# Planning a gated attention and MLP kernel again: modelled buffer slots, score bursts on distinct row tiles, copies from the first, one Gelu per batch

## The chip, the cores and the metric

The kernel runs on one core of one Trainium2 chip. The metric is the device time of one execution in microseconds (us). An engine is named as the profile names it: PE is the matmul engine, ACT is ScalarE, DVE is VectorE, POOL is GpSimd, SP is the engine that issues most DMAs.

## The reference, cut to what matters

```python
# x: 2048 x 512 (bf16), 32 heads of 16, F = 1792
qkv = (x @ wqkv) ...                                  # q, k, v per head
scores = einsum("bhqd,bhkd->bhqk", q, k) * 16 ** -0.5
a = einsum("bhqk,bhkd->bhqd", softmax(scores), v) ... @ wo

h  = gelu(layernorm(x) @ w1)                          # first Gelu batch
x1 = x + concat(four quarters of h, shifted by 1, -1, 2, -2 rows) @ w2
b  = x1 + gelu(layernorm(x1) @ w3) @ w4               # four more batches, one per 512 rows

g  = sigmoid((x * gate_w).sum(-1))
out = g * a + (1 - g) * b
```

Softmax over 32 heads x 2048 x 2048 scores is the bulk of the work. A *score tile* is 128 keys x 512 queries of one head; there are 2048 of them, handled in 32 rounds of 64 (a round is a chunk `c` of 512 queries, a group `G` of eight heads, and the even or odd heads `p` of the group). Each tile needs a small score matmul, an exp, and P·V matmuls that are collected in one accumulator, `acc`, in PSUM, the memory that PE writes to.

## The kernel before

The order of every instruction is planned at build time by an event model inside the kernel, the class `Sim`. It has one queue per engine, a duration and a latency for every job, and counts of free buffers. In this text "the planner" is that model. Once the chip runs, each engine works through its list in the planned order, so a wrong latency in the planner can't be corrected at run time.

Two parts matter here. The first is how a score tile becomes weights for P·V. Most tiles go to ACT as bursts of three or two tiles. About a quarter go to DVE, which builds an approximate exp from the bits: one pass `p1`, then two shifted copies on DVE and one on POOL. A tile done this way needs four P·V matmuls instead of one.

```python
def issue_act(got, cls):                      # 3 or 2 score tiles in one PSUM buffer
    ...
        nc.scalar.activation(out=box["p"][:, 0:n], in_=get()[:, 0:n], func=ACT.Exp, scale=0.25)

def act_tiles(n):                             # which tiles: distinct row groups within one burst
    for r in range(acc_round[0], min(NR, acc_round[0] + 3)):
        for x in left[r]:
            ...
            if any(g[1][1] == x[1] for g in got):
                continue
            got.append((r, x))
            if len(got) == n:
                return got

def close_pair(pr):                           # two DVE tiles together, 1024 wide
    ...
    for k in range(1, 4):
        def sh(k=k):
            d = pr["box"]["d"]
            if k < 3:                         # copy k reads copy k - 1
                nc.vector.tensor_scalar(out=d[:, k, 0:w], in0=d[:, k - 1, 0:w], scalar1=float(SHIFT), ...)
            else:
                nc.gpsimd.tensor_scalar(out=d[:, k, 0:w], in0=d[:, k - 1, 0:w], ...)
        j = dve(0.26 * w + 72.0, last, sh, prio=1) if k < 3 else gp(..., last, sh, prio=1)
        last = [j]
```

The second is the Gelu. It is cut into four instructions per batch, each with the previous one as a dependency, and only the first is charged with a table load by the planner:

```python
for m in range(KT):                           # first batch: KT = 4
    ge.append(act(1800 + (1300 if m == 0 else 0), pre + ge, lambda m=m: nc.scalar.activation(
        out=hT["h"][:, m, 2:2 + S], in_=hT["h"][:, m, 2:2 + S], func=ACT.Gelu_apprx_tanh), prio=0))
...
for q, (a, b) in enumerate(((0, 4), (4, 8), (8, 11), (11, 14))):    # in each of four chunks
    ge.append(act(93 + 427 * (b - a) + (1300 if q == 0 else 0), pre + ge, ...Gelu of box["h"][:, a:b, :]))
```

The third is the planner's constants, the buffer pools, and the gate, which writes one number per row to DRAM and reads it back in another layout:

```python
class Sim:
    SWITCH = 95.0
    ISSUE = 27.0
    PE_LAT = 220.0
...
NPA, NPD = 5, 3                               # exp results; DVE quadruples of [P, 4, 1024]
oDp = pool("oDp", 2)                          # attention output, [P, 4, 512] for a whole chunk c
...
d1 = dma(2200.0, [a], lambda: nc.sync.dma_start(out=zE_dram[:].rearrange("(t p) -> p t", p=P), in_=zE[:]))
...
# end of a round: acc -> accsb, its denominators -> den -> pk, then on DVE
r1 = dve(230, [d1], lambda: nc.vector.reciprocal(out=box["k"][:], in_=box["k"][:]), prio=0)
r2 = dve(90, [r1] + jg[1], ...pk * gpk...)    # gpk is the gate, read back from zE_dram
```

The softmax here doesn't subtract the row's maximum and nothing guards it: scores larger than these inputs give would overflow.

Of the kernel before, what the change touches and what calls it, by code (L numbers as in the profile page):

```python
# [18 lines left out]
SHIFT = 32  # L19
# [21 lines left out]
class Buf:  # L41
    def __init__(self, cls, users):
        self.cls, self.users = cls, users
# [34 lines left out]
class Sim:  # L78
    SWITCH = 95.0
    ISSUE = 27.0  # L80
    PE_LAT = 220.0

    def __init__(self, counts):
        self.free = dict(counts)
        self.jobs = {e: [] for e in ("ACT", "DVE", "POOL", "SP")}
        self.t_free = {e: 0.0 for e in ("ACT", "DVE", "POOL", "SP", "PE")}
        self.t = 0.0
        self.events = []
        self.n = 0
        self.order = []  # L90
        self.mode = None
        self.arr = [0.0] * 4
        self.tiles = 0
        self.pending = 0
        self.busy = {e: 0.0 for e in self.t_free}
        self.stat = {}
        self.log = []

# [10 lines left out]

    def release(self, bufs):  # L110
        for b in bufs:
            b.users -= 1
            if b.users == 0:
                self.free[b.cls] += 1
# [10 lines left out]
    def try_engine(self, e):  # L125
# [3 lines left out]
        for j in self.jobs[e]:  # L129
# [6 lines left out]
            if any(self.free[b.cls] <= 0 for b in j.acq):  # L136
                continue
# [7 lines left out]
        for b in j.acq:  # L145
            self.free[b.cls] -= 1
# [10 lines left out]
    def pe_run(self, ops):  # L157
        cur = self.t
        for o in ops:
# [11 lines left out]
            o.start = s  # L171
            cur = s
# [16 lines left out]
    def run(self, pe_pick, done):  # L189
# [17 lines left out]
        if not done():  # L207
            raise RuntimeError(f"the model of the engines stopped at {self.t}: {self.free} {self.tiles} {[(j.name,len(j.deps)) for e in self.jobs for j in self.jobs[e]][:20]}")
# [3 lines left out]
def kernel(  # L212
# [26 lines left out]
    COL = True  # L239

    NPA, NPD = 5, 3
    pool = lambda name, bufs, **kw: ctx.enter_context(tc.tile_pool(name=name, bufs=bufs, **kw))
    const = pool("const", 1)
    wpool = pool("wpool", 4)
    qpool = pool("qpool", 2)
    bigp = pool("bigp", 1)
    xnTp = pool("xnTp", 2)
    xnp = pool("xnp", 4)
    pap = pool("pap", NPA)
    pdp = pool("pdp", NPD)  # L250
    accp = pool("accp", 2)
    oTp = pool("oTp", 2)
    oDp = pool("oDp", 2)
    otp = pool("otp", 2)
    smallp = pool("smallp", 3)
    psA = pool("psA", 1, space=bass.MemoryType.PSUM)
    psR = pool("psR", 2, space=bass.MemoryType.PSUM)
    psC = pool("psC", 1, space=bass.MemoryType.PSUM)
    dpool = pool("dram", 1, space=bass.MemoryType.DRAM)
    drr = pool("drr", 3, space=bass.MemoryType.DRAM)  # L260
# [3 lines left out]


    x_sb = const.tile([P, NT, D], BF16, name="x_sb")
    xT = const.tile([P, KT, S], BF16, name="xT")
    wq = const.tile([P, KT, D], BF16, name="wq")
    wo = const.tile([P, KT, D], BF16, name="wo")
    w3 = const.tile([P, KT, F], BF16, name="w3")  # L270
    kT = [const.tile([P, S], BF16, name=f"kT{g}") for g in range(4)]
    V0 = const.tile([P, NT, 4, 4, 2, DH + 1], BF16, name="V0")
    V2 = const.tile([P, NT, 4, 2, 2, DH + 1], BF16, name="V2")
    gw = const.tile([P, KT], BF16, name="gw")
    mE = const.tile([P, 1], F32, name="mE")
    mO = const.tile([P, 1], F32, name="mO")
    mhalf = const.tile([P, NT], F32, name="mhalf")
    omg = const.tile([P, NT], F32, name="omg")
# [4 lines left out]
    nm = [const.tile([P, NT], F32, name=f"nm{i}") for i in range(2)]  # L283
    xn_dram = dpool.tile([2, S, D], BF16, name="xn_dram")
# [5 lines left out]
    sim = Sim({"psA3": 1, "psA2": 1, "ring": 2, "acc": 1, "PA": NPA, "PD": NPD, "xnT": 2, "xn": 4, "accsb": 2, "bcs": 2,  # L290
               "oT": 2, "q": 2, "qf": 2, "big": 1, "ot": 2, "small": 3, "w": 4, "oD": 2})
# [16 lines left out]
    wts = {}  # L308

    def wload(name, src, c0=0, c1=None):  # L310
        def fn():
            wts[name] = wpool.tile([P, KT, D], BF16, tag="w", name="w_" + name)
            n = src.shape[0] // P
            nc.sync.dma_start(out=wts[name][:, 0:n, :], in_=wrows(src))
        return fn

    wk_t = wpool.tile([P, KT, D], BF16, tag="w", name="w_k")
    wts["k"] = wk_t
    sim.free["w"] -= 1
    for c0, c1 in ((0, 128), (128, 512)):  # L320
        nc.scalar.dma_start(out=wk_t[:, :, c0:c1], in_=wrows(A_wqkv[:, D + c0:D + c1]))
        nc.scalar.dma_start(out=wq[:, :, c0:c1], in_=wrows(A_wqkv[:, c0:c1]))
    wv_t = wpool.tile([P, KT, D], BF16, tag="w", name="w_v")
    wts["v"] = wv_t
    sim.free["w"] -= 1
    nc.scalar.dma_start(out=wv_t[:], in_=wrows(A_wqkv[:, 2 * D:3 * D]))
    nc.scalar.dma_start(out=gw[:], in_=gate_w.rearrange("(kt p) -> p kt", p=P))
    dl_w = {"k": sim.add(Job("SP", 1, 5000.0, [], None)), "v": sim.add(Job("SP", 1, 9000.0, [], None))}

    gp(150, [], lambda: nc.gpsimd.memset(mhalf[:], -0.5), prio=0)  # L330

    mi = const.tile([P, 1], mybir.dt.int32, name="mi")
    mb = const.tile([P, 1], mybir.dt.int32, name="mb")
    gp(200, [], lambda: nc.gpsimd.iota(mi[:], pattern=[[0, 1]], base=0, channel_multiplier=1), prio=0)
    j_io = sim.jobs["POOL"][-1]
# [6 lines left out]
    gp(700, [], lambda: nc.gpsimd.memset(V0[:, :, :, :, :, 0:1], 1.0), prio=1)  # L342
    j_v1 = sim.jobs["POOL"][-1]

    acc = psC.tile([P, 512], F32, name="acc")
    j_acc0 = dve(550, [], lambda: nc.vector.memset(acc[:], 1.0), prio=0)

    j_xT = {}
    for c in range(NCH):
        for k in range(KT):  # L350
            j_xT[c, k] = dma(2600.0 + 300.0 * k, [], lambda c=c, k=k: nc.sync.dma_start(  # L351
                out=xT[:, k, c * 512:(c + 1) * 512], in_=x_by_d[c * 512:(c + 1) * 512, k], transpose=True), prio=0)
    j_x = []
    for c in range(NCH):
        j_x.append(dma(4000.0, [], lambda c=c: nc.sync.dma_start(
            out=x_sb[:, 4 * c:4 * c + 4, :], in_=x_flat[c * 512:(c + 1) * 512, :].rearrange("(t p) d -> p t d", p=P)),
            prio=1))
    bw = {}
    for name, src in (("1", B_w1), ("2", B_w2)):
        bw[name] = Buf("w", 0)  # L360
        dl_w[name] = dma(5000.0, [], wload(name, src), prio=2, acq=[bw[name]])
    dl_w["o"] = dma(5000.0, [], lambda: nc.sync.dma_start(out=wo[:], in_=wrows(A_wo)), prio=2)
    dl_w["3"] = dma(9000.0, [], lambda: nc.sync.dma_start(out=w3[:], in_=wrows(B_w3)), prio=2)
# [4 lines left out]
    def gen(name, at, deps, mms, N=512, M=P):  # L368

        box = {}  # L370

        def get():
            if "ps" not in box:
                box["ps"] = psR.tile([P, 512], F32, tag="ring", name="ring")
            return box["ps"]

# [11 lines left out]
        g.get = get  # L388
# [3 lines left out]
    def evac(g, hold, fn, prio=2, eng="DVE", **kw):  # L392
        job = Job(eng, hold, 150.0, [g.units[-1][-1]] if not COL else g.units[-1], lambda: fn(g.get()), prio=prio,
                  frees=[g.buf] + kw.pop("frees", []), **kw)
        return sim.add(job)
# [6 lines left out]
    def k_proj(G, c, at):  # L402
        g = gen(f"k{G}", at, [j_xT[c, k] for k in range(KT)] + [dl_w["k"]],
                [(lambda a, b, k=k: wts["k"][:, k, G * P + a:G * P + b],
                  lambda k=k: xT[:, k, c * 512:(c + 1) * 512]) for k in range(KT)])
# [4 lines left out]
    qt = {}  # L410
    j_q = {}

    qbuf = {}

    def q_proj(G, c, at):
        g = gen(f"q{G}", at, [j_xT[c, k] for k in range(KT)] + [dl_w["k"]],
                [(lambda a, b, k=k: wq[:, k, G * P + a:G * P + b],
                  lambda k=k: xT[:, k, c * 512:(c + 1) * 512]) for k in range(KT)])
        box = {}
        qfb = Buf("qf", 2)  # L420

        def cp(ps):
            box["f"] = qpool.tile([P, 512], BF16, tag="qf", name="qf")
            nc.vector.tensor_copy(out=box["f"][:], in_=ps[:])

        e = evac(g, PSUM_NS, cp, prio=1, acq=[qfb])
        qb = Buf("q", 128)
        qbuf[G, c] = qb
        js = []
        for p, m in ((0, mE), (1, mO)):  # L430
            def mk(p=p, m=m):
                if p == 0:
                    qt[G, c] = qpool.tile([P, 2, 512], BF16, tag="q", name="q")
                nc.gpsimd.tensor_scalar(out=qt[G, c][:, p, :], in0=box["f"][:], scalar1=m[:], scalar2=1.0,
                                        op0=ALU.mult, op1=ALU.mult)
            js.append(gp(680, [e, j_m3] + js, mk, prio=0, acq=[qb] if p == 0 else [], frees=[qfb]))
        j_q[G, c] = js
# [4 lines left out]
    def v_proj(t, at):  # L442
        c = t // 4
        g = gen("v", at, [j_xT[c, k] for k in range(KT)] + [dl_w["v"]],
                [(lambda a, b, k=k: xT[:, k, t * P + a:t * P + b], lambda k=k: wts["v"][:, k, :]) for k in range(KT)])
        j_v[t] = evac(g, PSUM_NS, lambda ps: nc.vector.tensor_copy(  # L446
            out=V0[:, t, :, :, :, 1:DH + 1], in_=ps[:].rearrange("p (g i o d) -> p g i o d", g=4, i=4, o=2)), prio=2)
        e = t % 2
        j_v2[t] = gp(480, [j_v[t], j_v1], lambda: nc.gpsimd.tensor_scalar(
            out=V2[:, t], in0=V0[:, t, :, e::2, :, :], scalar1=W2, scalar2=1.0, op0=ALU.mult, op1=ALU.mult), prio=1)  # L450


    def gate(at):
        g = gen("z", at, [j_xT[c, k] for c in range(NCH) for k in range(KT)], [], M=P)
# [683 lines left out]
```

## Time and profile before

| before | |
|---|---|
| time, median of its 4 runs beside the result | 954.03 us (951.48 to 961.69) |
| ACT busy / PE busy in the profiled run | 807.8 / 832.3 of 951.6 us |
| table loads on ACT | 41, of 1283 ns |
| ACT idle up to its last exp | 120.1 us |
| PE slots used by the 2048 score matmuls | 1016, of which 379 with one matmul |

The idle time of ACT is summed from the gaps between its instructions in the trace, and 807.8 + 120.1 + 23.8 us after the last exp gives the span, but for rounding. A *score slot*, or PE slot, is a group of score matmuls that start less than 60 ns after one another, because they use different row tiles of the array and run side by side; it is not one of the buffer slots below.

The profile page of the kernel before has the busy time of each engine, the busy tenths in 40 slices with the PE clock that was granted (PEclk, in tenths of full clock; "half clock" below is a stretch in which half was granted), and the chain of work that ended last.

```profile
PE 832.3 (87%) x8949; PEld 258.6 (27%) x8949; DVE 715.2 (75%) x1338; ACT 807.8 (85%) x680; POOL 386.9 (41%) x405
...
PE   4996899997789989978999987999959999979982
...
ACT  0665999999889999998979899799998889999990
...
PEclk9997999998799999976979997999968999969996
...
PE 51%; ACT 16%; DVE 16%; issue 8%; DMA 3%; SPq 3%; POOL 2%; ACTq 0%; POOLq 0%; DVEq 0%
```

No engine is full over the whole span. ACT does almost nothing in the first slice (23.8 us); afterwards ACT and PE take turns at 9. In the table of stretches (start:end, length, then the busy us of PE, PE weight load, DVE, ACT, POOL with their instructions, PE clock, DMA share, GB/s) the two regimes of the kernel before stand side by side:

```profile
192.00:240.00 48.00, 37.64 (x384) 10.91 (x381) 35.55 (x69) 46.54 (x39) 20.06 (x20) 0.93 0.09 27
...
480.00:528.00 48.00, 47.85 (x637) 16.95 (x633) 29.50 (x56) 39.90 (x34) 15.29 (x14) 0.93 0.10 27
```

In the first ACT is full (46.5 of 48), in the second PE is (47.9 of 48). Anything taken from ACT should pay at once in the first and not in the second. The groups of the kernel before by shape (line, engine, operation, shapes, count, then busy us and mean ns, then idle time just before and its releasers) show what fills ACT, and the DVE copies:

```profile
L732 ACT ACTIVATE PA<-psA 128x1536 bf16<-128x1536 f32 x309 | 452.5, 1464 | 75.4 <-PE psA L673 62.4 <-PE acc L820 9.0 <-PE ring L673 1.9
...
L792 DVE TENSOR_SCALAR PD<-PD 128x1024 uint16<-128x1024 uint16 x502 | 252.3, 503 | 10.6
...
L732 ACT ACT_TABLE_LOAD x21 | 26.9, 1283 | 11.3 <-DMA wq<-in_A_wqkv_dram 11.0
...
L600 ACT ACT_TABLE_LOAD x16 | 20.5, 1283 | 0.3
...
L557 ACT ACT_TABLE_LOAD x4 | 5.1, 1283 | 0.1
```

The three rows of loads are 21 + 16 + 4 = 41, or 52.6 us: 20 to a Gelu, 20 back to exp, and one at the start. The timeline of ACT (start, duration, engine, line, operation, count) in the kernel before shows why there are so many:

```profile
409.51 1.28 ACT L600 ACT_TABLE_LOAD   x1
410.81 1.91 ACT L600 ACTIVATE h<-h 128x2048 bf16<-128x2048 bf16 x1
412.74 1.28 ACT L732 ACT_TABLE_LOAD   x1
414.03 1.02 ACT L732 ACTIVATE PA<-psA 128x1024 bf16<-128x1024 f32 x1
415.07 1.28 ACT L600 ACT_TABLE_LOAD   x1
```

Between two quarters of one Gelu batch the planner slips a single exp of 1.02 us, and that costs two loads, 2.56 us. The code explains it: a quarter counts as finished 160 ns after it leaves ACT, so when ACT comes free the next quarter isn't ready yet, an exp is, and the planner does not charge the loads that this brings.

The waits of ACT for scores and P·V before (engine, tile and line, what was waited for: us in total, times, longest) come to 73.3 + 26.9 + 3.9 = 104 us; the page's own total for the exp, with small items, is 107.1 us.

```profile
ACT PA L732 <- PE psA L673: 73.3, 91, 12.1
ACT PA L732 <- PE acc L820: 26.9, 22, 3.5
...
ACT PA L732 <- PE ring L673: 3.9, 10, 0.9
```

Last, two places of the timeline before: the first exp, and one pair of shifted copies on DVE.

```profile
24.33 2.36 ACT L732 ACTIVATE PA<-psA 128x1536 bf16<-128x1536 f32 x2 [12.07 <-PE psA L673]
...
305.34 0.96 DVE L792 TENSOR_SCALAR PD<-PD 128x1024 uint16<-128x1024 uint16 x2
```

### The profile page before, as it was taken

What the parts mean: (1) busy time and instruction counts of PE and PEld (TensorE: products, weight loads), DVE (VectorE), ACT (ScalarE), POOL (GpSimd) and SP (SyncE); (2) the same over time, 40 slices, a digit from 0 to 9 for tenths busy, and PEclk for the clock granted to TensorE, in tenths of its full rate; (3) what the DMA queues carried; (4) which work ended last, traced back from release to release, by engine and by line L of the source; (5) the groups of instructions that cost most, each with busy time, mean ns of one, the idle gap of its engine ahead of it and who ended that gap; (6) DMA issues with size and microseconds to landing.
All of it is one profiled execution on the core that took longest, in us unless ns stands there. A gap on an engine that the chain in (4) does not pass through costs nothing.

```text
span 951.6 us, 22237 instructions
## 1 busy us (share of the span) xinstructions
PE 832.3 (87%) x8949; PEld 258.6 (27%) x8949; DVE 715.2 (75%) x1338; ACT 807.8 (85%) x680; POOL 386.9 (41%) x405
## 2 busy tenths in 40 slices
PE   4996899997789989978999987999959999979982
PEld 1341232322222223311223322332312333223220
DVE  1775988887699998856966785788848678857881
ACT  0665999999889999998979899799998889999990
POOL 1343653343367773423432342333424334324340
PEclk9997999998799999976979997999968999969996
DMA  7621221101012210010000010100000000000001
GB/s 157 231 58 32 76 61 28 48 18 38 4 50 60 61 37 17 15 26 15 17 22 26 22 32 9 33 20 17 15 3 16 28 25 16 17 4 16 16 18 37
DMA packets 64728, 34.27 MB, mean 36 GB/s; under 512 B 44784, under 2 KB 59888, under 8 KB 64624
## 3 DMA queue, kind: packets, MB, share of 16 engines
q1 hardware_dynamic: 61456, 31.27, 12.3%
q10 hardware_dynamic: 3168, 1.57, 0.7%
q8 instruction: 70, 1.15, 0.5%
q14 instruction: 34, 0.28, 0.1%
HBM read 17.60 MB, written 6.82 MB: 26 GB/s over the span
## 4 chain that ended last, share of the span: by engine, by line
PE 51%; ACT 16%; DVE 16%; issue 8%; DMA 3%; SPq 3%; POOL 2%; ACTq 0%; POOLq 0%; DVEq 0%
PE acc L820 17%; PE ring L381 15%; PE psA L673 12%; ACT PA L732 10%; DVE PD L769 7%; PE ring L673 6%; DVE PD L792 5%; ACT L732 3%; SPq L351 2%; ACT L600 2%; DMA zE_dram<-zE 1%; DVE st L483 1%; ACT h L600 1%; POOL PD L795 1%; DVE accsb L836 1%
## 5 line engine op out<-in xcount | busy, mean ns | idle before, releaser
L732 ACT ACTIVATE PA<-psA 128x1536 bf16<-128x1536 f32 x618 | 720.1, 1251 | 107.1 <-PE psA L673 73.3
L795 POOL TENSOR_SCALAR PD<-PD 128x1024 uint16<-128x1024 uint16 x252 | 263.6, 1046 | 466.7 <-DVE PD L792 300.9
L769 DVE TENSOR_SCALAR PD<-ring 128x512 uint16<-128x512 f32 x503 | 338.0, 683 | 146.9 <-PE ring L673 120.0
L820 PE MATMUL acc<-PD,V 128*17 128x512 bf16 x2012 | 309.6, 408 | 14.4 <-POOL PD L795 6.3
L673 PE MATMUL psA<-q,kT 32*128 32x512 bf16 x1545 | 247.7, 397 | 53.0 <-ACT PA L732 51.2
L820 PE MATMUL acc<-PA,V 128*17 128x512 bf16 x1545 | 266.9, 396 | 3.0 <-DVE V L446 1.2
L792 DVE TENSOR_SCALAR PD<-PD 128x1024 uint16<-128x1024 uint16 x504 | 253.6, 504 | 10.6
L673 PE MATMUL ring<-q,kT 32*128 32x512 bf16 x503 | 185.4, 403 | 15.2 <-DVE kT L406 8.6
L673 PEld LDWEIGHTS <-kT 32*128 32x128 bf16 x2048 | 79.8, 92 | 303.9 <-issue 299.4
L820 PEld LDWEIGHTS <-V 128*17 128x17 bf16 x3557 | 91.9, 90 | 248.1 <-issue 211.7
L381 PE MATMUL ring<-xnT,w 128*32 128x512 bf16 x1152 | 86.5, 381 | 0.5 <-DVE PD L769 0.2
L381 PE MATMUL ring<-w,h 128*32 128x512 bf16 x896 | 67.7, 398 | 0.6 <-DVE ot L629 0.4
L875 POOL TENSOR_TENSOR oT<-accsb,bcs 128x512 bf16<-128x512 f32 x32 | 41.5, 1297 | 28.1 <-DMA bcs<-rr 24.1
L594 DVE CAST h<-ring 128x512 bf16<-128x512 f32 x56 | 38.2, 684 | 5.0 <-PE ring L381 4.6
L381 PEld LDWEIGHTS <-w 128*32 128x32 bf16 x1152 | 30.8, 96 | 33.2 <-issue 16.8
L381 PE MATMUL ring<-xT,w_k 128*32 128x512 bf16 x256 | 25.2, 469 | 13.4 <-DMA xT<-in_A_x_dram 13.0
L732 ACT ACT_TABLE_LOAD x21 | 26.9, 1283 | 11.3 <-DMA wq<-in_A_wqkv_dram 11.0
L381 PEld LDWEIGHTS <-h 128*32 128x32 bf16 x896 | 27.0, 100 | 29.2 <-issue 13.9
L510 POOL TENSOR_SCALAR xn<-x_sb,rs,nm 128x512 bf16<-128x512 bf16 x32 | 27.5, 865 | 2.6 <-DVE nm L499 2.2
L600 ACT ACTIVATE h<-h 128x2048 bf16<-128x2048 bf16 (+1 forms) x16 | 27.1, 1696 | 0.2
L406 DVE CAST kT<-ring 128x512 bf16<-128x512 f32 x16 | 11.0, 686 | 20.9 <-PE ring L381 20.9
L836 DVE COPY accsb<-acc 128x512 f32<-128x512 f32 x32 | 21.8, 681 | 3.0 <-PE acc L820 2.9
(51 smaller groups left out, 317.9 us busy)
## 6 DMA issues: line engine op xcount, KB each, us to landing
bcs<-rr SPq DMA_DIRECT2D x128, 64.0 KB
xn_dram<-xn SPq DMA_DIRECT2D x32, 128.0 KB
w<-in_B_w_dram SPq DMA_DIRECT2D x5, 512.0 KB
x_sb<-in_A_x_dram SPq DMA_DIRECT2D x4, 512.0 KB
oD<-oT SPq DMA_DIRECT2D x128, 16.0 KB
out_dram<-ot SPq DMA_DIRECT2D x16, 128.0 KB
w<-in_B_w_dram SPq DMA_DIRECT2D x1, 1792.0 KB
w_v<-in_A_wqkv_dram ACTq DMA_DIRECT2D x1, 512.0 KB
```

The lines of the kernel that those rows point to most:

```text
L381: units.append([Op("col", j, lambda j=j, lf=lf, rf=rf, st=st, sp=sp: nc.tensor.matmul(get()[32 * j:32 * j + 32, 0:N], lhsT=lf(32 * j, 32 * ...
L510: nc.gpsimd.tensor_scalar(out=box["x"][:], in0=x_sb[:, t, :], scalar1=rs[which][:, t:t + 1], scalar2=nm[which][:, t:t + 1], op0=ALU.mult, ...
L594: nc.vector.tensor_copy(out=box["h"][:, m, :], in_=ps[:])
L600: ge.append(act(93 + 427 * (b - a) + (1300 if q == 0 else 0), pre + ge, lambda a=a, b=b: nc.scalar.activation(out=box["h"][:, a:b, :], in_ ...
L673: o = Op("row", i, lambda: nc.tensor.matmul(dst(), lhsT=kT[G][32 * i:32 * i + 32, kt * P:(kt + 1) * P], rhs=qt[G, c][32 * i:32 * i + 32, p ...
L732: nc.scalar.activation(out=box["p"][:, 0:n], in_=get()[:, 0:n], func=ACT.Exp, scale=0.25)
L769: nc.vector.tensor_scalar(out=pr["box"]["d"][:, 0, h * 512:(h + 1) * 512], in0=get()[:], scalar1=BITS_MUL, scalar2=BITS_ADD, op0=ALU.mult, ...
L792: nc.vector.tensor_scalar(out=d[:, k, 0:w], in0=d[:, k - 1, 0:w], scalar1=float(SHIFT), scalar2=None, op0=ALU.add)
L795: nc.gpsimd.tensor_scalar(out=d[:, k, 0:w], in0=d[:, k - 1, 0:w], scalar1=1.0, scalar2=float(SHIFT), op0=ALU.mult, op1=ALU.add)
L820: o = Op("col", i, lambda: nc.tensor.matmul(acc[32 * i:32 * i + DH + 1, :], lhsT=lhs(), rhs=rhs(), start=st, stop=True, tile_position=(0, ...
L836: nc.vector.tensor_copy(out=box["a"][:], in_=acc[:])
L875: nc.gpsimd.tensor_tensor(out=box["o"][:], in0=box["a"][:], in1=box["b"][:], op=ALU.mult)
```

## The change

The intent: cut the table loads by making each Gelu batch one instruction; pack score matmuls better by giving the tiles that start together distinct row tiles of the array; let the planner hand out *fixed slots* of buffers in the order in which its model frees them, in place of pools that rotate; correct its constants; start exp sooner by loading x in the order in which it is needed; and let both DVE copies read the first tile instead of each other. DVE now takes only even key tiles and ACT prefers odd ones, which halves the scaled copy of V. The diff cut to its core:

```diff
 class Sim:
     SWITCH = 95.0
-    ISSUE = 27.0
-    PE_LAT = 220.0
+    ISSUE = 4.0
+    PE_LAT = 275.0
 ...
-    NPA, NPD = 5, 3
+    NPA, NPD, NW = 6, 16, 9
 ...
-    sim = Sim({"psA3": 1, "psA2": 1, "ring": 2, "acc": 1, "PA": NPA, "PD": NPD, ..., "oD": 2})
+    sim = Sim({
+        ...
+        "PA": slots("PA", NPA, [P, 1536]),
+        "PD": slots("PD", NPD, [P, 1024], U16),      # one slot per copy, freed one by one
+        "oD": slots("oD", 6, [P, 512]),              # one slot per (c, G)
+        ...
 ...
-            j_xT[c, k] = dma(2600.0 + 300.0 * k, [], ...)
+            j_xT[c, 0, k] = load_xT(c, k, 0, 2600.0 + 1150.0 * (4 * c + k + 1), 0)
 ...
-        for m in range(KT):
-            ge.append(act(1800 + (1300 if m == 0 else 0), pre + ge, lambda m=m: ...))
+        ge = act(93 + 1700 * KT + 2600, pre, lambda: nc.scalar.activation(
+            out=hT[:, :, 2:2 + S], in_=hT[:, :, 2:2 + S], func=ACT.Gelu_apprx_tanh), prio=0)
 ...                                                  # and the same in each chunk: 7168 wide, once
-                    nc.vector.tensor_scalar(out=d[:, k, 0:w], in0=d[:, k - 1, 0:w], scalar1=float(SHIFT), ...
+                    nc.vector.tensor_scalar(out=d[k][:, 0:w], in0=d[0][:, 0:w], scalar1=float(SHIFT * k), ...
 ...
+                j = dve(0.26 * w + 72.0, pr["jobs"], sh, prio=1, acq=[bufs[k]], frees=[bufs[0]])
 ...
-                got = act_tiles(int(cls[-1]))
+            got = act_tiles(w, used if len(used) + w <= 4 else set())
 ...
-                x = dve_tile()
+                x = dve_tile(used if len(used) < 4 else set())
```

Left out: the rewriting of every allocation as a slot, twelve more transposed loads of x, a new rule for how many P·V matmuls to batch, and when to load w3 and w4.

## The prediction

> **What bounds the kernel now.** Two engines in turn. The page: span 951.6 us, ACT busy 807.8 (85%), PE 832.3 (87%), DVE 75%, POOL 41%. In the table of stretches ACT is full in the Gelu stretches (46.5 us of 48 at 192-240, 46.2 at 384-432) while PE is light there (half clock from 415 to 446 us); where projections are dense PE is full (47.9 of 48 at 480-528) and ACT drops to 39. The chain of waits: PE 51%, ACT 16%, DVE 16%. ACT's exp waits 107 us: 73 on scores, 27 on a PE still in P·V. In the first 24 us ACT does almost nothing.
>
> **What the change removes.**
> 1. *Table loads.* By line, ACT has 41 ACT_TABLE_LOADs of 1283 ns, 52.6 us (the Trainium skill, "ScalarE: Activation LUTs", What ACT_TABLE_LOAD costs, also says 1283 ns, plus a drain); the timeline shows every one of 20 Gelus between two loads. Five Gelus need about 11: 30 x 1.29 = 39 us, 42 with lost overlap. These stretches are ACT-bound, so I count 34. Against it: exp stops for 9-10 us at once (4 x 1.9 + 2 x 1.28), PE runs dry and its clock halves.
> 2. *Score slots.* Grouping score matmuls that start together, 2048 scores take 1016 slots of 216-228 ns, 379 of them with one matmul. Distinct row tiles should bring 750-800: 50 us of PE. A change between score and P·V shape takes 317-323 ns start to start instead of 216 ("TensorEngine Tiling (Array Packing)", Key Properties: a mode change drains), 1106 times, 110 us; longer P·V batches should cut 10-20%.
> 3. *Model.* Starts within a slot are 3 ns apart, where the model had 27; slots follow its release order, not a rotating pool's; PD is freed per copy, PA has 6 for 5. ACT's wait on PE (100 us) should fall by a third to a half.
> 4. *Start.* The old model lets all transposed loads land at about 3 us; the trace has one each 1.3 us until 22 us, and as K of all chunks is queued ahead, the first exp starts at 24.3 us. The new order should start it at 12-16: 7 us.
> 5. *Shifted copies* both read the first: a shorter chain to POOL, same DVE work (504 copies, 254 us).
>
> **What it adds.** 12 more transposed loads (1.15 us of the SP queue each), off the path.
>
> **Sum.** ACT needs 720 us of exp (1545 tiles, 466 ns each) + 35 Gelu + 14 tables = 769. Before, it was 89% busy between 24 and 912 us; with PE relieved I take 92-93%: 830, plus 16 of start and 28 of tail gives 874. A few more tiles on DVE take 466 ns each from ACT. I predict **872 us**, 840 to 912 in 8 of 10. Chances: faster by over 2% 0.93, within 2% 0.05, slower 0.02.
>
> **What would show it.** About 11 table loads; ACT busy about 770, 88% of the span; its waits on scores and P·V below 70; single-matmul score slots well under 379, mode changes under 1000; first exp before 16 us; half clock still after each Gelu; DVE about 80%.
>
> **What would make it wrong.** The long Gelu leaves PE idle and at half clock for 20-30 us each time, so that refilling scores eats the saved loads; distinct-tile and fill rules starve DVE or make P·V late, so that ACT waits for PA; the even-key rule unbalances DVE; slots make a hidden dependency (large h buffer, x reload) that stalls an engine; the model's remaining errors leave real waits as they were.

## The result

The kernel after took 891.3 us (median of 4 runs, 889.26 to 893.4) against 954.03 us: ratio 0.933, with a 95% interval of 0.9271 to 0.9389. A ratio is the mean time of one kernel's runs over that of the kernel before's runs of the same rounds, so it is not quite the ratio of the medians. The predicted 872 was 19 us too low; 891.3 lies inside the range of 840 to 912, and "faster by over 2%" came true. The gain was 62.7 us where 82 had been predicted, so about three quarters of it.

The page after, for the same lines:

```profile
PE 786.6 (89%) x8981; PEld 251.1 (28%) x8982; DVE 693.1 (78%) x1361; ACT 755.7 (85%) x631; POOL 390.5 (44%) x400
...
PE   5996899898898989979898998999988999989982
...
ACT  3364999899998999998993998999998889999990
...
PEclk9987999999799999988999996999978999979996
...
PE 48%; ACT 23%; DVE 12%; issue 7%; DMA 4%; POOL 4%; SPq 2%; POOLq 0%; ACTq 0%; DVEq 0%
```

ACT's busy time fell by 52.1 us, and its idle time up to the last exp from 120.1 to 109.3, by 10.8. The tail after the last exp stayed (23.8 and 23.9). These two falls are the whole gain of 62.7 us of span. So four fifths of it is work that ACT no longer does, and one fifth is waiting that it no longer does. Of the 52.1 us, 38.5 are the loads, 3.0 are the Gelus themselves (five are shorter than twenty: 32.0 in place of 35.0 us), and 10.4 are exps, half of them because DVE took 11 tiles more (514 in place of 503). The busy share of ACT is 85% in both kernels: a share does not show a gain that shortens the numerator and the span alike. One digit is new in ACT's row, the 3 near the middle (slice 22, from 467 to 489 us).

The groups after, by shape:

```profile
L741 ACT ACTIVATE PA<-psA 128x1536 bf16<-128x1536 f32 x307 | 451.8, 1472 | 81.8 <-PE ring L665 31.5 <-PE acc L821 30.1 <-PE psA L665 18.8
...
L790 DVE TENSOR_SCALAR PD<-PD 128x1024 uint16<-128x1024 uint16 x514 | 219.5, 464 | 6.3 <-PE acc L821 0.7
...
L600 ACT ACTIVATE hT<-hT 128x7168 bf16<-128x7168 bf16 x4 | 24.7, 6177 | 0.0
...
L741 ACT ACT_TABLE_LOAD x6 | 7.7, 1283 | 11.4 <-DMA wq<-in_A_wqkv_dram 11.3
...
L600 ACT ACT_TABLE_LOAD x4 | 5.1, 1283 | 0.1
L567 ACT ACT_TABLE_LOAD x1 | 1.3, 1283 | 0.0
```

There are 6 + 4 + 1 = 11 loads, 30 fewer. The exps themselves are the same within 0.6% (1472 ns against 1464). The copies on DVE take 464 ns on average instead of 503, with the same shape. The timeline of ACT after shows a whole Gelu batch between two loads, 8.7 us without exp:

```profile
389.22 1.28 ACT L600 ACT_TABLE_LOAD   x1
390.51 6.18 ACT L600 ACTIVATE hT<-hT 128x7168 bf16<-128x7168 bf16 x1
396.71 1.28 ACT L741 ACT_TABLE_LOAD   x1
```

The waits of ACT after are nearly as long in sum, 38.4 + 32.9 + 24.7 = 96 us, but of another kind:

```profile
ACT PA L741 <- PE acc L821: 38.4, 14, 14.6
ACT PA L741 <- PE ring L665: 32.9, 62, 2.2
ACT PA L741 <- PE psA L665: 24.7, 26, 9.5
```

The waits on score bursts fell from 73.3 to 24.7 us. The waits under PE ring, where the last thing before the exp was a score for DVE, rose from 3.9 to 32.9. The waits on P·V rose from 26.9 to 38.4, and one of them is 14.6 us long. Here it is, in the timeline after:

```profile
472.76 2.37 ACT L741 ACTIVATE PA<-psA 128x1536 bf16<-128x1536 f32 x2 [0.43 <-PE acc L821]
...
483.12 5.07 SPq L855 DMA_DIRECT2D oD<-oT  x8
...
486.38 1.27 POOL L851 TENSOR_TENSOR oT<-accsb,bcs 128x512 bf16<-128x512 f32 x1 [6.43 <-DMA oD<-oT]
...
488.22 0.68 DVE L834 COPY accsb<-acc 128x512 f32<-128x512 f32 x1
...
489.70 1.45 ACT L741 ACTIVATE PA<-psA 128x1536 bf16<-128x1536 f32 x1 [14.58 <-PE acc L821]
```

Read it from below. ACT waits for P·V to free an exp buffer; P·V waits for `acc` to be copied out to `accsb`; that waits for POOL to free `accsb`; POOL waits for its output `oT` to be copied on into `oD`; and that copy starts only at 483 us, because no `oD` slot was free. The change turned two `oD` buffers of four quarters (8 quarters) into 6 single quarters. The quarters of chunk 0 are held until its last four projections have run, which the plan puts at score tiles 1045 to 1080, so the next chunk has two slots where it had four.

The first exp and one pair of DVE copies, in the timeline after:

```profile
12.56 2.37 ACT L741 ACTIVATE PA<-psA 128x1536 bf16<-128x1536 f32 x2
...
303.64 0.74 DVE L790 TENSOR_SCALAR PD<-PD 128x1024 uint16<-128x1024 uint16 x2
```

The first exp comes 11.8 us earlier (12.56 instead of 24.33). Two copies take 0.74 us in place of 0.96 in these examples. And one old wait is still there, in the timeline of DVE after:

```profile
69.26 0.66 DVE L766 TENSOR_SCALAR PD<-ring 128x512 uint16<-128x512 f32 x1
77.86 0.25 DVE L841 RECIPROCAL pk<-pk 128x16 f32<-128x16 f32 x1 [7.95 <-DMA pk<-den]
...
80.85 0.44 DVE L842 TENSOR_TENSOR pk<-pk,gpk 128x16 f32<-128x16 f32 x1 [1.53 <-DMA gpk<-zE_dram]
```

DVE stands for 7.95 us before a reciprocal of 0.25 us, because the small load `pk<-den` is late, and ACT soon stands too, for 9.52 us from 73 us on (9.59 us in the kernel before). At that time the gate is written to DRAM, 2048 values of 4 bytes, in 11.25 us; the planner was told 2.2. The chain of waits after has it as one step (start, duration):

```profile
66.39 11.25 DMA zE_dram<-zE
```

### The profile page after: what moved, and what is told of

Same layout as the page of the kernel before. It is cut to its first block, busy times and chain, and to the rows that moved or that the text cites. A ratio compares the mean times of both kernels' runs of the same rounds, so it can differ in the third digit from the quotient of the medians.

```text
span 888.9 us, 22112 instructions
## 1 busy us (share of the span) xinstructions
PE 786.6 (89%) x8981; PEld 251.1 (28%) x8982; DVE 693.1 (78%) x1361; ACT 755.7 (85%) x631; POOL 390.5 (44%) x400
## 4 chain that ended last, share of the span: by engine, by line
PE 48%; ACT 23%; DVE 12%; issue 7%; DMA 4%; POOL 4%; SPq 2%; POOLq 0%; ACTq 0%; DVEq 0%
ACT PA L741 18%; PE acc L821 17%; PE ring L411 17%; PE psA L665 11%; DVE PD L766 5%; DVE PD L790 3%; ACT hT L600 3%; PE ring L665 3%; POOL PD L793 2%; DMA zE_dram<-zE 1%; DVE st L509 1%; POOL xn L529 1%; SPq L364 1%; ACT hT L567 1%; DMA w<-in_A_x_dram 1%
## 5 line engine op out<-in xcount | busy, mean ns | idle before, releaser
L741 ACT ACTIVATE PA<-psA 128x1536 bf16<-128x1536 f32 x614 | 709.7, 1259 | 97.8 <-PE acc L821 38.4
L821 PE MATMUL acc<-PD,V 128*17 128x512 bf16 x2056 | 328.8, 401 | 25.4 <-DVE PD L790 10.5
L821 PE MATMUL acc<-PA,V 128*17 128x512 bf16 x1534 | 292.7, 389 | 2.8 <-DVE accsb L834 2.0
L790 DVE TENSOR_SCALAR PD<-PD 128x1024 uint16<-128x1024 uint16 x514 | 219.5, 464 | 6.3 <-PE acc L821 0.7
L411 PE MATMUL ring<-w,hT 128*32 128x512 bf16 x1152 | 84.0, 387 | 1.5 <-DVE x_sb L576 0.8
L411 PEld LDWEIGHTS <-w 128*32 128x32 bf16 x1664 | 45.2, 98 | 56.4 <-issue 32.9
L851 POOL TENSOR_TENSOR oT<-accsb,bcs 128x512 bf16<-128x512 f32 x32 | 41.1, 1283 | 25.1 <-DMA bcs<-rr 18.7
L598 DVE CAST hT<-ring 128x512 bf16<-128x512 f32 x56 | 38.4, 685 | 9.7 <-PE ring L411 9.2
L411 PE MATMUL ring<-w,w 128*32 128x512 bf16 x512 | 44.5, 430 | 1.6 <-DVE PD L766 0.8
L411 PEld LDWEIGHTS <-hT 128*32 128x32 bf16 x1152 | 30.2, 97 | 36.7 <-issue 18.4
L411 PE MATMUL ring<-w,wq 128*32 128x512 bf16 x256 | 20.8, 395 | 8.1 <-DMA w<-in_A_x_dram 6.9
L600 ACT ACTIVATE hT<-hT 128x7168 bf16<-128x7168 bf16 x4 | 24.7, 6177 | 0.0
L509 DVE BATCH_NORM_STATS2 st<-x_sb 128x6 f32<-128x512 bf16 x32 | 21.7, 679 | 0.1
```

What stands on the lines that cost most here:

```text
L411: units.append([Op("col", j, lambda j=j, lf=lf, rf=rf, st=st, sp=sp: nc.tensor.matmul(get()[32 * j:32 * j + 32, 0:N], lhsT=lf(32 * j, 32 * ...
L509: a = dve(600, deps, lambda: nc.vector.bn_stats(out=sb.slot[:], in_=x_sb[:, t, :]), prio=6, at=at, acq=[sb])
L598: pre.append(evac(g, PSUM_NS, lambda ps, m=m: nc.vector.tensor_copy(out=h2[:, m, :], in_=ps[:]), acq=[bb] if m == 0 else []))
L600: ge = act(93 + 427 * FT + 2600, pre, lambda: nc.scalar.activation(out=h2, in_=h2, func=ACT.Gelu_apprx_tanh), prio=0)
L741: job = act(hold, ops, lambda: nc.scalar.activation(out=pb.slot[:, 0:n], in_=buf.slot[:, 0:n], func=ACT.Exp, scale=0.25), acq=[pb], frees= ...
L790: nc.vector.tensor_scalar(out=d[k][:, 0:w], in0=d[0][:, 0:w], scalar1=float(SHIFT * k), scalar2=None, op0=ALU.add)
```

## The experiments

All twelve kernels gave the correct result, and each was timed in 4 runs. The expectations number the theories; in words they are these. The gain is mostly table loads (T1), or mostly better packing of the scores on PE (T2). The hole at 475 us comes from the `oD` slots (T3), or from PE full of projections (T4). The planner's new constants (T5) and the larger exp buffers (T6) carry part of the gain. The wait at the gate comes from a small load that lies behind the gate's write in the SP queue (T7), from PE (T8), from waiting for the gate itself (T9), or from DMA engines that all queues share (T10). Reading both copies from the first tile saves DVE time that is worth 25 us in either kernel (T11), or is worth that only with the new slots or by the way in which it was undone (T12).

The times of the kernel before were 959.98, 961.91, 957.79 and 958.37 us on three chips, so kernels are compared by their ratios, and a difference of ratios is given as a share of the time of the kernel before (1% is 9.6 us).

### A change that should do nothing

Any edit of the planner's inputs gives another order of 22,000 instructions, so this control tells how far time moves without a cause. It changes one duration by 10 ns.

```diff
-    PSUM_NS = 600.0
+    PSUM_NS = 610.0
```

> The changed kernel with one model number moved that should mean nothing: a PSUM eviction is planned with 610 ns instead of 600. It measures how far a time moves because the plan comes out differently. If plans are as good as equal, the ratio is 0.931 to 0.935; if a plan is worth some microseconds of luck, as the two gate runs suggest (3 us better with the hole gone, 5 us better with it still there), it may lie anywhere in 0.927 to 0.939, and no effect below about 6 us that I measured can be put down to its cause by the time alone.

It took 890.8 us, ratio 0.9311 [0.9244, 0.9377], against 0.933 of the kernel after. DVE got 504 tiles instead of 514, and the gaps moved (104.9 us of ACT idle instead of 109.3), but the time did not. I take from it, and from the widths of the intervals, that an effect under about 1% can't be put down to an edit by its time alone.

### The Gelu, from both sides

On the kernel after, the Gelu was cut into quarters again:

```diff
-        ge = act(93 + 1700 * KT + 2600, pre, lambda: ...Gelu of hT[:, :, 2:2 + S]...)
+        gl = []
+        for m in range(KT):
+            gl.append(act(1800 + (1300 if m == 0 else 0), pre + gl, lambda m=m: ...Gelu of hT[:, m, 2:2 + S]...))
+        ge = gl[-1]
 ...                                                  # and in each chunk (0, 4), (4, 8), (8, 11), (11, 14)
```

> The changed kernel with the Gelus cut into 4 per batch again (20 instructions, one exp free to slip in after each). Theory T1 (most of the gain is ACT work, 28-30 table loads less): 41 table loads again, ACT busy back to about 795, time 891 + 35 to 42 = 926 to 933 us. Rival T2 (the gain is the PE side: better slots and a truer model; ACT had slack): within 10 us of the changed kernel, 881 to 901 us.

And on the kernel before, it was merged, with nothing else changed:

```diff
-        for m in range(KT):
-            ge.append(act(1800 + (1300 if m == 0 else 0), pre + ge, ...))
+        ge.append(act(93 + 1700 * KT + 2600, pre, lambda: ...Gelu of hT["h"][:, :, 2:2 + S]...))
 ...                                                  # and in each chunk once over box["h"][:]
```

> The kernel before with one Gelu per batch and nothing else. T1: 11 table loads, ACT busy about 765, 954 minus 34 to 42 = 912 to 920 us. T2: the long Gelu only starves PE and the rest stays PE-bound: 940 to 955 us.

Cutting it again took 938.38 us, ratio 0.9767 [0.9715, 0.9819]: 0.0437 above the kernel after, or 42 us of the 960 that the kernel before took. Merging alone took 920.22 us, ratio 0.9574 [0.9521, 0.9628], 40 us less than the kernel before. The number of loads went to 41 and to 11 as expected. Both sides agree on 40 to 42 us, two thirds of the whole gain. Thirty loads fewer, so each was worth about 1.35 us. In the trace of the merged kernel ACT's busy time fell by 44.1 us: 38.5 for the loads, 3.0 for the shorter Gelus and 2.5 for exps; its idle time up to the last exp rose by 5.8.

The prediction took 8 us off this term, since a longer Gelu should leave PE idle and at half clock for longer. The records of the granted clock say the opposite. Time below full clock within the span, summed, was 150.7 us before, 109.3 with the Gelu merged alone, 99.4 after, and 152.1 after with the Gelu cut again. A batch in quarters stretched over a longer time in which exp came one at a time, and PE ran at half clock through it, up to 30.7 us at one piece. Merged, the longest such piece after a Gelu is 13.7 us in the kernel after, and 20.5 us with the Gelu merged alone.

### Distinct row tiles

On the kernel after, the tiles that start together need no longer be on distinct row tiles (within one burst they still are):

```diff
-            got = act_tiles(w, used if len(used) + w <= 4 else set())
+            got = act_tiles(w, set())
...
-                x = dve_tile(used if len(used) < 4 else set())
+                x = dve_tile(set())
```

> The changed kernel with score matmuls of different buffers free to share a row tile again (each burst of one buffer stays distinct). Row slots go back towards 950, single-matmul slots towards 300. T1 (ACT and its waits for other causes bound it): at most 8 us slower, 888 to 899 us. T2 (PE slots are worth it): 15 to 40 us slower, 906 to 931.

It took 900.1 us, ratio 0.9372 [0.9326, 0.9418], 0.4% above the kernel after, and the intervals overlap: the two together leave room for anything from no loss to 11 us. T2 is out; the time of 900.1 us lies just above T1's range of 888 to 899. The scores took 886 slots in place of 772, with 258 singles in place of 144, and PE was 12.4 us busier (799.0 against 786.6). So the rule does what it was made for, but a cost of 12 us on PE moved the time by about 4 us. It is also not the whole of the better packing: a little over half of the way from 1016 slots to 772 is there without the rule (886). Where that half comes from, no run isolates; the version below with the old constants needs 744 slots, so it is not the constants.

### The `oD` slots

```diff
-        "oD": slots("oD", 6, [P, 512]),
+        "oD": slots("oD", 8, [P, 512]),
...
-    zero = const.tile([P, 512], BF16, name="zero")   # never read
-    j_z = dve(300, [], lambda: nc.vector.memset(zero[:], 0.0), prio=0)
```

> The changed kernel with 8 quarter slots of the packed attention output instead of 6 (the kernel before had 2 tiles of 4 quarters), room made by dropping a tile of zeros that nothing reads. Theory T3: the 14.6 us hole of ACT at 475 us is a chain of full buffers: chunk 1's third group finds no oD slot until chunk 0's last w4 has run, so oT, bcs, accsb, acc and PA fill up and exp stops. Then the hole goes and the time falls by 11 to 15 us, to 876 to 881. Rival T4: the hole is PE saturated by the w4 and w3 matmuls that stand there; they stay, so the hole stays at 8 us or more and the time at 886 to 893.

It took 889.48 us, ratio 0.9248 [0.9185, 0.9311], 0.8% under the kernel after. The hole is gone, as the timeline of this kernel shows for the same place:

```profile
466.51 6.88 ACT L739 ACTIVATE PA<-psA 128x1536 bf16<-128x1536 f32 x6 [1.15 <-PE acc L819]
473.89 9.27 ACT L739 ACTIVATE PA<-psA 128x1536 bf16<-128x1536 f32 x8 [0.49 <-PE ring L663]
```

A hole of 10.9 to 16.1 us at this place is in the trace of every version with 6 slots, and in none with 8, so its cause is settled. Its worth is not its length. Between the two profiled runs ACT's idle time fell by 6.1 us, not by 14, and ACT was busy for 4.4 us more since DVE had taken 506 tiles instead of 514. During the hole PE had done projections, which now have to find another place; that they compete with scores there is not shown. The gain of 7 us was below the 11 to 15 expected, 889.48 us even lies in the range that T4 had given, and a gain of 0.8% is within what the control allows. It is the trace that decides for T3, not the time.

### The planner's constants, and the exp buffers

```diff
-    ISSUE = 4.0
-    PE_LAT = 275.0
+    ISSUE = 27.0
+    PE_LAT = 220.0
...
-    DVE_STOP, DVE_ALONE, SL3, SL2, PD_LOW = 6, 0, 250.0, 500.0, 1
+    DVE_STOP, DVE_ALONE, SL3, SL2, PD_LOW = 6, 0, 120.0, 120.0, 1
```

> The changed kernel planned with the old model numbers: 27 ns between starts in a slot (4), 220 ns PE latency (275), slack of 120 ns before the next scores (250 and 500). The changed kernel is 0.933 of before. Theory T5 (what is left of the gain after the Gelus, about 16 us, comes mostly from these numbers: longer P.V batches, fewer slots, less order that PE cannot keep): 8 to 16 us slower, ratio 0.941 to 0.950, ACT's idle time up by about as much. Rival T6 (it comes from the buffers): ratio 0.930 to 0.938.

It took 896.98 us, ratio 0.9346 [0.9307, 0.9385], 0.2% above the kernel after. T5 fell: the corrected constants carry no gain that can be measured here.

```diff
-    NPA, NPD, NW = 6, 16, 9
+    NPA, NPD, NW = 5, 12, 9
```

> The changed kernel with 5 PA slots (6) and 12 PD slots (16), the capacity of the kernel before. T6 (the buffers carry the rest of the gain): 8 to 16 us slower, ratio 0.941 to 0.950. T5 (the model numbers do): at most 5 us slower, 0.930 to 0.938. Both can be partly right.

It took 902.95 us, ratio 0.9404 [0.9348, 0.946], 0.7% or 7 us above, between the ranges of T5 and T6. The intervals overlap and the control limits what can be said: the direction fits T6, the size is uncertain.

### The wait at the gate

First, only the latency that the planner assumes for the gate's write was corrected, on top of the 8 slots:

```diff
-        d1 = dma(2200.0, [a], lambda: nc.sync.dma_start(out=zE_dram[:].rearrange(...), in_=zE[:]))
+        d1 = dma(11500.0, [a], lambda: nc.sync.dma_start(out=zE_dram[:].rearrange(...), in_=zE[:]))
```

> The version with 8 oD slots, gate at tile 50, only its write told to the model as 11.5 us instead of 2.2. The product that waits for the gate moves back in VectorE's queue, but the small load of the reciprocal still lies behind the scattered write in the DMA queue: T7 says that VectorE still stands there 7 to 8 us, hole of ACT 6 us or more, time within 3 us of 8 slots alone (ratio 0.921 to 0.928). If the wait for the gate itself were the cause (rival T9), the hole would shrink below 3 us and the ratio fall to 0.915 to 0.919.

It took 882.1 us, ratio 0.9192 [0.9153, 0.9231], but the wait stayed: the reciprocal stood for 10.68 us and ACT for 11.1. The planner had moved the product behind other work, as it should, but not the reciprocal, whose load it believes to take 2 us. So it is not the wait for the gate itself (T9). The time was 5 us better than with the 8 slots alone, where at most 3 had been expected; this run does not show why, and 0.6% is within what the control allows.

Then the gate was started earlier as well, while DVE has other work to do:

```diff
-    jg = gate(50)
+    jg = gate(20)
```

> The version with 8 oD slots, with the gate's matmuls at score tile 20 instead of 50 and its scattered write told to the model as 11.5 us. Theory T7: ACT's 8 to 9 us hole at 74 us is VectorE standing in its queue: a reciprocal waits for a small load that lies in the DMA queue behind the gate's 2048 four-byte writes (11 us), then the product waits for the gate. With the gate early, VectorE never stands there; the hole goes, 6 to 9 us faster than with 8 slots alone (0.9248): ratio 0.915 to 0.919. Rival T8: the hole is PE short of work at half clock and full of projections; they only move: within 3 us, 0.922 to 0.928.

Now DVE never stands for long there and the hole in ACT at 74 us is gone, as T7 said. Yet the time was 887.82 us, ratio 0.9265 [0.9215, 0.9315], no better than the 8 slots alone and in T8's range. In place of the hole ACT has two new pauses, of 6.5 us at 45 us and of 4.2 us at 53 us, before exps that wait for P·V. The lead was real and was given back: score tile 128 started at 86.1 us instead of 92.5 (the version with 8 slots), tile 512 at 235.9 instead of 249.0, tile 1024 at 443.3 instead of 450.9, and the last at 858.6 instead of 861.5. An early gain of 13 us shrank to 3.

Last, the write of the gate was issued by ACT's queue, so that it should not delay the small loads of the SP queue:

```diff
-        d1 = dma(2200.0, [a], lambda: nc.sync.dma_start(out=zE_dram[:]..., in_=zE[:]))
+        d1 = sim.add(Job("ACT", 420, 11500.0, [a], lambda: nc.scalar.dma_start(out=zE_dram[:]..., in_=zE[:])))
```

> 8 oD slots, gate at tile 50 as in the change, the gate's scattered write issued from ScalarE's DMA queue and told to the model as 11.5 us. T7 (the reciprocal's small load stood behind the scattered write in SyncE's DMA queue): now it need not, VectorE's wait of 8 to 11 us before the first reciprocal falls below 3 us, ACT's hole at 71 to 82 us below 4 us, and the time falls 4 to 9 us below the same kernel with the write on SyncE's queue (0.9192): ratio 0.910 to 0.915. Rival T10 (the scattered write slows every small transfer whatever its queue, because the 16 DMA engines are shared): VectorE still waits 6 us or more there, ratio 0.917 to 0.923.

The delay stayed, though shorter. The chain of waits of this version has the small write that had taken 1.7 to 2.5 us at other times in the run, now at the gate:

```profile
63.70 9.71 DMA den<-accsb
...
368.36 1.68 DMA den<-accsb
```

DVE waited for 6.80 us and ACT for 7.2. So the other queue does not take the write out of the way, which is T10, and the time is in T10's range. The Trainium skill, "DMA: Bandwidth & Descriptors", Issuing engines are not separate DMA queues, says that DMAs of all issuing engines interleave on the same 16 DMA engines; this trace agrees, with 9.71 us in place of 1.68. Even so it is the fastest version: 879.23 us (877.77 to 882.89), ratio 0.9175 [0.9126, 0.9223]. That is no credit to the queue: the first of these three versions, with the write on the SP queue, has 0.9192 and the intervals overlap. It beats both kernels; against the control the medians are 879.23 and 890.8, 1.3% apart, and the runs do not overlap.

### The shifted copies, from both sides

On the kernel after, each DVE copy read the one before it again:

```diff
-                    nc.vector.tensor_scalar(out=d[k][:, 0:w], in0=d[0][:, 0:w], scalar1=float(SHIFT * k), ...
+                    nc.vector.tensor_scalar(out=d[k][:, 0:w], in0=d[k - 1][:, 0:w], scalar1=float(SHIFT), ...
...
-                j = dve(0.26 * w + 72.0, pr["jobs"], sh, prio=1, acq=[bufs[k]], frees=[bufs[0]])
+                j = dve(0.26 * w + 72.0, last, sh, prio=1, acq=[bufs[k]], frees=[bufs[k - 1]])
```

> The changed kernel with the second shifted copy made from the first copy again instead of from the original. VectorE runs its queue in order and the copies stand next to each other, so its work is the same (0.76 us for two). I expect no effect beyond the luck of the plan: ratio 0.928 to 0.938. If the shorter chain to GpSimd mattered, P.V of the shifted copies would come later and PD would run out: 0.940 or more.

On the kernel before with the Gelu merged, both copies read the first:

```diff
-                    nc.vector.tensor_scalar(out=d[:, k, 0:w], in0=d[:, k - 1, 0:w], scalar1=float(SHIFT), ...
+                    nc.vector.tensor_scalar(out=d[:, k, 0:w], in0=d[:, 0, 0:w], scalar1=float(SHIFT * k), ...
...
-            j = dve(0.26 * w + 72.0, last, sh, prio=1) if k < 3 else ...
+            j = dve(0.26 * w + 72.0, pr["jobs"], sh, prio=1) if k < 3 else ...
```

> The kernel before with two edits only: one Gelu per batch (ratio alone 0.9574) and the second shifted copy made from the first like the change does. Theory T11 (undoing the copies cost 25 us because a copy that reads the one just written starts 461 ns after it instead of 342, 119 ns for each of 252 pairs, 30 us of VectorE, and ScalarE then waits for score buffers that VectorE holds): ratio 0.925 to 0.938, as fast as the whole change. Start distance of the pair 340 to 350 ns, copies 220 us busy. Rival T12 (the 25 us came from how I undid it in the slot accounting, or the gain needs the new slots): 0.945 to 0.960.

Chaining them again, where I had expected no effect, took 918.76 us, ratio 0.9587 [0.9537, 0.9638], 2.6% above the kernel after and 28 us above the control. The page, waits and groups of that kernel show where:

```profile
PE 48%; DVE 24%; ACT 11%; DMA 5%; issue 4%; SPq 3%; POOL 2%; POOLq 0%; DVEq 0%; ACTq 0%
...
L790 DVE TENSOR_SCALAR PD<-PD 128x1024 uint16<-128x1024 uint16 x520 | 258.7, 498 | 17.3 <-DVE PD L790 0.5
```

```profile
ACT PA L741 <- PE ring L665: 58.9, 75, 6.9
```

DVE has 24% of the chain in place of 12%, and ACT's wait under PE ring is 58.9 us in place of 32.9. Part of the mechanism can be read from the starts in the trace. Where the two copies of a pair stand next to each other on DVE, the second starts 461 ns after the first in the kernel before (median; 144 of its 251 pairs), 342 ns after it in the kernel after (228 of 257), and 343 ns in the kernel before with this edit (226 of 249). A copy lasts 426 ns there, so an independent one starts before the first has ended, and a dependent one cannot. In the other pairs the plan puts another instruction between the two, because it counts a dependent copy as ready only 150 ns after the first has ended. So the 119 ns hold for 144 pairs of the kernel before, or 17 us, and not for all 252, or 30 us, as T11 has it. In the kernel after with the copies chained, 104 of 259 pairs are parted, and in the rest the second starts 523 ns after the first.

The copies' busy time on DVE (1024 wide) fell by 31 us in one test (251.2 to 219.8) and by 38 in the other (257.4 to 219.5). Of either, about 19 us are the overlap of two copies. Most of the rest is that fewer copies are slow: 52 in place of 77, and 39 in place of 76, take over 600 ns. Every one of these runs at the same time as an instruction on POOL, and only one in seven or eight of the others does. The edit does one thing more: the copy on POOL starts 0.95 us after the first in place of 1.40, and 0.92 in place of 1.48 (medians), so that P·V of these tiles can come sooner. This is the rival that the expectation of the first run names, and it isn't separated from DVE's time.

In the kernel before, with the Gelu merged, the same edit took 911.74 us, ratio 0.9497 [0.9456, 0.9537], against 0.9574 of the merged Gelu alone: 0.8%, which is within what the control allows. T11 had expected 0.925 to 0.938, so there it fell, and T12's range held. So DVE saves much in both kernels, and the worth is not the same: about 7 us in one, 25 in the other. In the first, most of what DVE saved became idle time (198.6 to 220.3 us), mainly in waits for scores from PE; in the second, little did (190.7 to 195.8). I can't settle why. It may be that DVE's time counts for more where PE has been relieved; but DVE's share of the chain does not show it, as it falls in both (21% to 15%, and 24% to 12%), and it is 21% in the version with the old constants, which lost nothing measurable. Or my undoing also costs through the way in which the chained copies hold their slots, or through the other order.

## Why the prediction was right or wrong

**The main mechanism held.** The table loads fell to 11 as predicted, and they are worth 40 to 42 us, measured on both kernels, where 34 had been taken. The Trainium skill, "ScalarE: Activation LUTs", What ACT_TABLE_LOAD costs, has 1283 ns for the load, which the trace shows to the nanosecond; the drain that it adds to every switch isn't seen in the cost here (1.35 us per load). "Against it: ... PE runs dry and its clock halves" had the wrong sign. The Trainium skill, "TensorE: Matmul & The Clock Gate", What's actually happening, says that PE drops to half clock after an idle window of about 3.4 us. In this trace PE need not stand still for that: half clock does follow the start of each of the five merged Gelus, but in the 3.4 us before it sets in PE is busy for 1.8 to 2.5 us, as the profile models it, and never pauses for more than 1.3 us. Still the merging shortened the total from 150.7 to 109.3 us (99.4 in the kernel after), and the long pieces at half clock that are gone lay where the quarters had kept PE short of work.

**The step that failed: "Before, it was 89% busy between 24 and 912 us; with PE relieved I take 92-93%".** ACT was busy for 746.3 of the 840 us from 24 to 864, or 88.8%, as before. At 92.5% the same work would have taken 807 us, 33 less. ACT's work itself was 13 us below the predicted 769 (755.7), and that hid part of the miss: 5 us since DVE took 11 tiles more, which the prediction had named without counting them, 3 since five Gelus are shorter than twenty, and 5 since an exp took 463 ns a tile in place of 466. So that 872 was only 19 us off is in part luck. "Its waits on scores and P·V below 70" is the same step: they were 97.8 us, after 107.1 before. What the runs showed in place of it: a new wait of 14.6 us on `oD` slots, which the prediction named only in general ("slots make a hidden dependency") because I had not seen that the old pool counts whole chunks and the new one quarters; the old wait of 9.5 us at the gate, which was in the kernel before too and which I had not reckoned with at all; and many short waits that changed their kind and not their sum. Removing the first paid 0.8%, less than its length. Removing the second by an earlier gate paid nothing on top. So the two holes are 24 us of the missing 33 as they stand in the trace, but not as time that comes back: the rest of the plan takes most of it, and no run here brought the short waits down as a whole. That ACT stays near 89% is shown. The fastest version, with 8 slots and the right latency of the gate's write, comes to 90.7% between 24 us and its last exp; what would lift it to 92 or 93% is open.

**Score slots.** 1016 became 772, within the predicted 750 to 800, and singles fell to 144. PE's busy time fell by 45.7 us, near the 50 predicted, but not for the predicted reason alone: 11 to 14 us of it come with the merged Gelu, where less of PE's work runs at half clock (832.3 to 818.7 with the Gelu merged alone; 786.6 to 797.6 with it cut again). The rule alone is 12.4 us, and undoing it moved the time by 0.4%, within the intervals. The mode changes, "should cut 10-20%", rose from 1106 to 1171; each still takes about 320 ns start to start (median) instead of 216.

**Model.** ACT's wait on PE was to fall by a third to a half and fell by 9% (107.1 to 97.8 us). The constants alone are worth nothing measurable; the buffers perhaps 7 us.

**Start.** The first exp came at 12.56 us, at the early end of "12-16". By score tile 128 the lead was 5.5 us (98.0 became 92.5), by tile 512 it was 16. About 6 us of the early lead is the start, close to the predicted 7, but no run isolates it.

**Shifted copies: "same DVE work" was wrong.** The copies' busy time fell by 34 us: about 18 since the second of a pair no longer waits for the first and overlaps it, and about 16 since fewer of them are slow (39 over 600 ns in place of 78). Undone on the kernel after, this costs 25 to 28 us; done on the kernel before it brought 7. I had not counted it at all.

**The sum.** Gelu 40 to 42 us, copies 7 to 28, buffers 7, start about 6, slots of scores about 4, constants nothing, and minus 7 for the missing `oD` slots; all but the first, and the copies on the kernel after, are within what the control allows. These do not add up to a single figure, as the copies show, and their span includes the 62.7 us measured. The split of the keys into even and odd had no run of its own and stays untested.

## What to carry to other kernels

Count table switches before counting matmul efficiency: a single short exp between two parts of a Gelu costs two loads, and merging the parts was worth more than all packing of the array. Let derived copies read the original and not one another, since a dependent copy started later even on its own engine (461 against 342 ns here); and when a pool is re-cut into slots, compare the capacity in the same unit and look for who holds a slot longest. Relief on one engine turns into time only where it ended a wait, so predict the waits that are left, and, in a kernel planned ahead, check the planner's latencies against the trace (2.2 us against 11).

## What the Trainium skill lacked or had wrong

- "ScalarE: Activation LUTs", What ACT_TABLE_LOAD costs: it counts 2.66 us for every switch, load and drain. Here 30 switches fewer were worth 40 to 42 us, or about 1.35 us each, of which 0.1 us is the shorter Gelus, and in the timeline a load begins within 20 ns of the end of the instruction before it (404.80 + 4.69 = 409.49, load at 409.51).
- "VectorE: DVE Perf Modes", The DRAIN you can't avoid: it says that a row of copies takes the same time with a semaphore after each as with one after the last, and also that a next operation that is not held starts earlier. Here the two differ: a copy of 1024 uint16 that reads the output of the copy before it starts 461 ns after it, one that does not starts 342 ns after it (medians of neighbours). The section does not give these 119 ns, which came to 17 us in the 144 such pairs of the kernel before.
- "DMA: Bandwidth & Descriptors", Why small descriptors are slow (HBM only): it gives an overhead per packet, and no figure for elements written one by one. Here 2048 values of 4 bytes, 8 KB in all, took 11.25 us, and a small write beside them took 9.71 us instead of 1.68.
- "TensorEngine Tiling (Array Packing)", Key Properties: it says that a change of mode drains PE, and gives no figure. Here it costs about 100 ns: medians of 317 to 323 ns start to start, against 216.
- "TensorE: Matmul & The Clock Gate", What's actually happening: it doesn't say how idle PE has to be in an idle window. Here half clock set in after windows of 3.4 us in which PE was busy for 1.8 to 2.5 us (five Gelus of the kernel after).
